# A spectral filter beside a gated MLP: the complex product made whole before the way back, and the inverse rows taken through memory

## The chip, the cores and the metric

The kernel runs on one core of a Trainium2 chip. The metric is the device time of one execution in microseconds (us). The engines are named as in the profile: PE is TensorE's matmul, PEld its weight load, DVE is VectorE, ACT is ScalarE, POOL is GpSimd and SP is SyncE, which issues nearly all transfers (DMAs). They run side by side; each takes its own instructions in order and waits on semaphores.

## The reference

```python
x = A_x                                   # (1, 2048, 512), bf16
xn = _layernorm(x, axis=-1)
# _A_ref: spectral filter
X = jnp.fft.rfft2(xn.astype(jnp.float32), axes=(-2, -1))
X = X * (w_r + 1j * w_i)                  # (2048, 257)
A = jnp.fft.irfft2(X, s=(2048, 512), axes=(-2, -1)).astype(jnp.bfloat16)
# _B_ref: GeGLU
g = jnp.einsum("bsd,df->bsf", xn, w_gate) # w_gate, w_up: (512, 1792)
u = jnp.einsum("bsd,df->bsf", xn, w_up)
B = jnp.einsum("bsf,fd->bsd", _gelu(g) * u, w_down)
return x + A + B
```

The output is the input plus a two-dimensional Fourier filter of the normalized input plus a gated MLP of it.

## The kernel before, in words

The 2048 rows lie as 16 tiles (index j) of 128 partitions. The MLP is cut into units for PE. A GeGLU unit (`geglu_unit`, line 490) makes 128 hidden features of 512 rows: four matmuls of 512 columns for the gate and four for the up projection (L504), the GELU on ACT (L516) and the product with the up half on DVE into hT (L524). A down unit (`down_unit`, L552) is fourteen matmuls of 512 columns for one tile of rows, added to x by DVE (L558). After the first tiles, 66 such units are left in one list; `filler(n)` issues the next n of it. They are written by hand between the units of the spectral path, so that PE has work while that path waits for other engines. There is no planner: the order in which the program issues operations is the order on every engine, and dependencies become semaphore waits.

The spectral path factors the transform of length 2048 into 64 times 32 parts. `unit_A` (L574) and `unit_d` (L600), sixteen each, transform along the long factor and along the columns; the result goes to memory and back in two parts (`shuffle`, L619), which swaps the order of the indices. Then comes the loop that the change rewrites. It has 16 units of two groups each (32 groups, 257 columns of the half spectrum):

- `unit_B(u)` does two matmuls (L635) with the constant BM, which finish the forward transform. ACT copies the pair of PSUM banks to Xc (L640). DVE multiplies Xc by the real filter into M1 (L643) and by the imaginary one into M2 (L644).
- `unit_c(u)` does, for each group, two matmuls that add in one bank: one constant times M1 (L656), another times M2 (L657). The second constant holds the turn by the imaginary unit, so the complex product becomes whole only in this sum. ACT copies the pair to Vp (L662), and four transfers per unit (L667) spread it over the partitions of V.

A row of Xc holds one of four components (real or imaginary part, of a frequency or of its mirror) of one of 2 times 16 indices; before the change the component lies in the low bits of the row number (`row_c`, line 89). Sixteen `unit_e` (L683) and sixteen `unit_fin` (L704) go back along the two axes, and DVE and POOL add the result to x (L714 to L722). Every finished tile is stored by SP (L536).

The loop has 18 passes; pass u issues `unit_c(u - 2)`, `unit_B(u)` and one or two fillers, 19 in all. Two more fillers follow, then the loop over `unit_e` and `unit_fin` with one filler in each of 16 passes, and four down units at the end. PSUM has 8 banks: three for the GeGLU units, four for the spectral units, one for the down units. Xc, M1, M2 and Vp have two buffers each. The transfers of V wait for Vp and for the last `unit_A`, because V shares its buffer with `unit_A`'s input.

Of the kernel before, what the change touches and what calls it, by code (L numbers as in the profile page):

```python
# [8 lines left out]
ALU = mybir.AluOpType  # L9
# [23 lines left out]
def _build_constants():  # L33
# [26 lines left out]

    AM = np.zeros((P, NJ, P))
# [3 lines left out]
    for j in range(NJ):  # L65
        th = pi2 * np.outer(16.0 * p + j, e) / S
        AM[:, j, 0:64] = np.cos(th)
        AM[:, j, 64:128] = -np.sin(th)
        AM[:, j, 64] = alt
        EM[0:64, j, :] = 2.0 * np.cos(th.T)  # L70
        EM[64:128, j, :] = -2.0 * np.sin(th.T)
        EM[0, j, :] = 1.0
        EM[64, j, :] = alt

# [8 lines left out]
    def idx(comp, e2):  # L83
        return slice(comp * 32 + e2 * 16, comp * 32 + e2 * 16 + 16)
# [4 lines left out]
    def row_c(comp, e2):  # L89
        return 8 * jj + comp * 2 + e2  # L90
# [26 lines left out]

    CM = np.zeros((P, 2, 2, P))
    wi = np.conj(w)
    for kind in range(2):  # L120
        M = CM[:, kind, 0, :]
# [19 lines left out]
        for e2 in range(2):  # L141
            for re, im in ((0, 1), (2, 3)):
                CM[row_c(re, e2), kind, 1, :] = M[row_c(im, e2), :]
                CM[row_c(im, e2), kind, 1, :] = -M[row_c(re, e2), :]

# [8 lines left out]
class _Sched:  # L154
# [14 lines left out]
    def total(self, stream):  # L169
        return (stream, self.stream_cnt[stream])  # L170
# [59 lines left out]
def bass_parallel_sum__spectral_gfnet__glu_gated_geglu__prompt_kernel(  # L230
# [21 lines left out]
    with ExitStack() as es:  # L252

        def sb(name, shape, dt=BF16):
            return es.enter_context(nc.sbuf_tensor(name, shape, dt))
# [22 lines left out]
        Xc = [sb("Xc%d" % i, [P, 2, NK]) for i in range(2)]  # L278
        M1 = [sb("M1_%d" % i, [P, 2, NK]) for i in range(2)]
        M2 = [sb("M2_%d" % i, [P, 2, NK]) for i in range(2)]  # L280
# [18 lines left out]
        CM = small[:, 3 * P:7 * P].rearrange("p (k t q) -> p k t q", k=2, t=2)  # L299
# [18 lines left out]
        def sp_bank_bf(slot):  # L318
# [12 lines left out]
                                      "w0", "w1", "w2", "w3", "dr0", "dr1", "perm1", "perm2_0", "perm2_1", "out")]  # L331
# [42 lines left out]
        d1 = nc.dram_tensor("stage_p", [NJ, P, 512], BF16).ap()  # L374

        def load_filter(name, dst, src):
            for q in range(4):
                e2 = q % 2
                load(name, dst[q:P:8, :, :], src.rearrange("(c h) k -> c h k", h=P)[:, 32 * e2:32 * e2 + 32, :])

                g0 = 1 - e2
                mirror = bass.AP(tensor=src.tensor, offset=src.offset + (P - 32 * e2 - g0) * NK,
                                 ap=[[P * NK, 16], [-NK, NG - g0], [1, NK]])
                load(name, dst[q + 4:P:8, g0:NG, :], mirror)
                if e2 == 0:
                    load(name, dst[q + 4:P:8, 0, :], src.rearrange("(c h) k -> c h k", h=P)[:, 64, :])
            spec[name] = [total(name)]
# [234 lines left out]
        Xc_readers = [[], []]  # L622
        M_readers = [[], []]
        Vp_readers = [[], []]
        ev_M = {}

        def unit_B(u):
            s2 = u % 2
# [11 lines left out]
            ev_c = sch.op("act", lambda e: e.activation(Xc[s2][:], sp_pair(slot), ACT.Copy), deps=[ev_p] + Xc_readers[s2])  # L640
            ring_sp.add_reader(slot, ev_c, 2)
            md = [ev_c] + M_readers[s2]
            a = sch.op("dve", lambda e: e.tensor_tensor(M1[s2][:], Xc[s2][:], wr_sb[:, 2 * u:2 * u + 2, :], ALU.mult), deps=md + spec["wr"])  # L643
            b = sch.op("dve", lambda e: e.tensor_tensor(M2[s2][:], Xc[s2][:], wi_sb[:, 2 * u:2 * u + 2, :], ALU.mult), deps=md + spec["wi"])  # L644
            Xc_readers[s2] = [a, b]
            ev_M[u] = [a, b]

        def unit_c(u):
# [3 lines left out]
            def f_c(e):  # L652
                ins = None
                for i in range(2):
                    kind = 1 if 2 * u + i == 0 else 0
                    e.matmul(sp_bank(slot + i)[:, 0:NK], CM[:, kind, 0, :], M1[s2][:, i, :], start=True, stop=False)  # L656
                    ins = e.matmul(sp_bank(slot + i)[:, 0:NK], CM[:, kind, 1, :], M2[s2][:, i, :], start=False, stop=True)  # L657
                return ins

            ev_p = sch.op("pe", f_c, deps=ev_M[u] + bdeps)  # L660
# [3 lines left out]
            for i in range(2):  # L664
                g = 2 * u + i
                for pq in range(2):
                    sch.op("sp", lambda e, g=g, i=i, pq=pq: e.dma_start(V[g:P:32, :, pq * HD:(pq + 1) * HD],  # L667
                                                                       Vp[s2][pq * 64:pq * 64 + 64, i, pq:pq + HD]),
                           deps=[ev_v, spec["A_last"]], stream="perm2_%d" % s2)
            Vp_readers[s2] = [total("perm2_%d" % s2)]  # L670
            spec["perm2_%d" % s2] = total("perm2_%d" % s2)
# [5 lines left out]
        def unit_e(j):  # L677
# [8 lines left out]
            ev_p = sch.op("pe", f_e, deps=[spec["perm2_0"], spec["perm2_1"], spec["eg"]] + bdeps)  # L686
# [123 lines left out]
        filler(5)  # L810

        spare = todo["left"] - 18 - 2 - 16 - 4
        for u in range(18):
            if u >= 2:
                unit_c(u - 2)
            if u < 16:
                unit_B(u)
            filler(1 + (u + 1) * spare // 18 - u * spare // 18)
        filler(2)
# [58 lines left out]
```

## Time and profile before

| | |
|---|---|
| median of 3 runs | 186.47 us (186.15 to 186.47) |
| the profiled execution | 186.33 us |
| its span, first to last instruction | 184.5 us |
| busy PE / DVE / ACT / POOL in the span | 180.1 / 109.6 / 88.0 / 55.4 us |
| `unit_B` matmuls L635 | 32 |
| `unit_c` matmuls L656, L657 | 32 and 32, 7.9 us of records each |
| products L643, L644 | 16 each, 428 and 422 ns |
| ACT copies Xc L640, Vp L662 | 16 each, 595 and 599 ns |
| transfers Vp to V (L667) | 64, 32.0 KB each |
| first `unit_B` to the end of the last `unit_c` | 77.35 to 121.21 us |

The busy times overlap, since the engines run side by side. Records of matmuls overlap as well: a matmul's record is longer than the distance to the next one's start, so the distances between starts tell what one costs. A line of the waits names who waited, for whom, and then the us in total, the number of times and the longest. A line of the order of time has the start, the length, the engine, the line and the operation, and in brackets the idle time before it with what ended it. The transfers' lines end in the number of issues, the KB of each and the median us from issue to landing.

### The profile page before, as it was taken

The page shows a single profiled execution, that of the slowest core. Times are in us where ns is not written, and L with a number is a line of the kernel's source. Part 1 is how long each engine was busy: PE and PEld are TensorE (multiplying, and loading weights), DVE is VectorE, ACT ScalarE, POOL GpSimd, SP SyncE. Part 2 cuts the span into 40 slices and gives each one's busy share as a digit, 9 for nine tenths or more (in the row PEclk, how much of TensorE's full clock was granted, in tenths as well). Part 3 has the DMA queues.
Part 4 walks back from the last instruction along what each step waited for, and adds up shares of the span by engine and source line. Part 5 has one row for each costly group of instructions (what it writes and reads, how often), then busy time and mean ns, then how long its engine had stood idle before and what let it go on. Part 6 is the DMA issues. An engine that isn't in the chain of part 4 may idle for free.

```text
span 184.5 us, 3257 instructions
## 1 busy us (share of the span) xinstructions
PE 180.1 (98%) x1197; PEld 103.6 (56%) x1197; DVE 109.6 (59%) x232; ACT 88.0 (48%) x161; POOL 55.4 (30%) x54
## 2 busy tenths in 40 slices
PE   7999999999999999999999999999999999998994
PEld 7788455565655544455555555554455555555453
DVE  2768968798674624365464654623266768688421
ACT  2644357777462633165475464523263635566000
POOL 0073290393720000000000000000049679699900
PEclk9999999999999999999999999999999999999999
DMA  5999972999994918301112112111001110111001
GB/s 152 352 365 373 373 233 82 164 189 262 197 203 153 290 64 236 134 0 52 46 47 52 51 50 54 46 41 27 5 0 57 54 63 28 57 59 34 28 28 57
DMA packets 25441, 21.95 MB, mean 119 GB/s; under 512 B 1617, under 2 KB 24657, under 8 KB 25297
## 3 DMA queue, kind: packets, MB, share of 16 engines
q1 hardware_dynamic: 24752, 21.32, 42.4%
q10 hardware_dynamic: 672, 0.43, 0.8%
q8 instruction: 9, 0.15, 0.4%
q14 instruction: 8, 0.06, 0.1%
HBM read 15.45 MB, written 4.19 MB: 106 GB/s over the span
## 4 chain that ended last, share of the span: by engine, by line
PE 93%; DMA 4%; SPq 1%; ACT 0%; issue 0%; DVE 0%
PE ps L504 51%; PE ps L552 26%; DMA wu_sb<-in_B_w_up_dram 4%; PE ps L574 2%; PE ps L683 2%; PE ps L600 2%; PE ps L635 2%; PE ps L657 2%; PE ps L656 2%; PE ps L704 2%; PE ps L441 2%; SPq L338 1%; ACT bufA L688 0%; DVE x_sb L558 0%
## 5 line engine op out<-in xcount | busy, mean ns | idle before, releaser
L504 PE MATMUL ps<-xnT,wg_sb 128*128 128x512 bf16 (+1 forms) x248 | 58.6, 359 | 0.3 <-DMA wu_sb<-in_B_w_up_dram 0.2
L504 PE MATMUL ps<-xnT,wu_sb 128*128 128x512 bf16 (+1 forms) x248 | 58.5, 359 | 0.0
L524 DVE TENSOR_TENSOR hT<-ps,gg 128x512 bf16<-128x512 f32 (+1 forms) x62 | 39.4, 637 | 19.7 <-PE ps L504 18.2
L552 PE MATMUL ps<-wd_sb,hT 128*128 128x512 bf16 (+1 forms) x238 | 50.5, 367 | 0.0
L516 ACT ACTIVATE gg<-ps 128x512 bf16<-128x512 f32 (+1 forms) x62 | 34.5, 556 | 23.2 <-PE ps L504 22.1
L718 POOL TENSOR_TENSOR bufC<-bufC 128x256 bf16<-128x256 f32 x16 | 14.7, 917 | 88.3 <-DVE bufC L715 88.3
L504 PEld LDWEIGHTS ps<-xnT,wu_sb 128*128 128x128 bf16 x248 | 24.2, 98 | 24.1
L552 PEld LDWEIGHTS ps<-wd_sb,hT 128*128 128x128 bf16 x238 | 22.9, 98 | 22.6
L504 PEld LDWEIGHTS ps<-xnT,wg_sb 128*128 128x128 bf16 x248 | 22.9, 98 | 15.8 <-DMA wu_sb<-in_B_w_up_dram 0.5
L558 DVE TENSOR_TENSOR x_sb<-ps,x_sb 128x512 bf16<-128x512 f32 (+1 forms) x17 | 11.2, 660 | 26.1 <-PE ps L552 26.1
L722 POOL TENSOR_TENSOR x_sb<-x_sb,bufC 128x512 bf16<-128x512 bf16 x16 | 18.7, 1169 | 2.3
L465 POOL TENSOR_TENSOR bufC<-bufA 128x1024 bf16<-128x1024 bf16 x8 | 16.8, 2124 | 7.9 <-DVE bufA L423 7.9
L662 ACT ACTIVATE Vp<-ps 128x514 bf16<-128x514 f32 x16 | 9.6, 599 | 19.1 <-DMA bufB<-Vp 10.9
L688 ACT ACTIVATE bufA<-ps 128x512 bf16<-128x512 f32 x16 | 9.6, 597 | 16.3 <-PE ps L683 16.3
L608 ACT ACTIVATE bufA<-ps 128x512 bf16<-128x512 f32 x16 | 11.9, 744 | 9.2 <-PE ps L600 9.2
L643 DVE TENSOR_TENSOR M<-Xc,wr_sb 128x514 bf16<-128x514 bf16 x16 | 6.9, 428 | 15.4 <-ACT Xc L640 15.4
L400 DVE BATCH_NORM_STATS2 st<-x_sb 128x6 f32<-128x512 bf16 x16 | 10.9, 680 | 2.4 <-DMA x_sb<-in_A_x_dram 2.3
L640 ACT ACTIVATE Xc<-ps 128x514 bf16<-128x514 f32 x16 | 9.5, 595 | 4.0 <-PE ps L635 4.0
L714 DVE TENSOR_TENSOR bufC<-bufC,ps 128x256 f32<-128x256 f32 x16 | 6.7, 421 | 5.7 <-ACT bufC L711 5.7
L657 PE MATMUL ps<-M,small 128*128 128x257 bf16 x32 | 7.9, 274 | 0.0
L656 PE MATMUL ps<-M,small 128*128 128x257 bf16 x32 | 7.9, 274 | 0.0
L415 POOL TENSOR_SCALAR rstd<-ag 128x4 f32<-128x4 f32 (+1 forms) x4 | 1.6, 402 | 20.4 <-DVE ag L401 20.4
(42 smaller groups left out, 142.5 us busy)
## 6 DMA issues: line engine op xcount, KB each, us to landing
stage_p<-bufA SPq DMA_DIRECT2D x16, 128.0 KB, 5.9
bufC<-stage_p SPq DMA_DIRECT2D x4, 512.0 KB, 5.0
bufB<-Vp SPq DMA_DIRECT2D x64, 32.0 KB
out_dram<-x_sb SPq DMA_DIRECT2D x15, 128.0 KB, 1.7
wd_sb<-in_B_w_down_dram SPq DMA_DIRECT2D x1, 1792.0 KB, 14.2
wr_sb<-in_A_w_r_dram SPq DMA_DIRECT2D x6, 257.0 KB, 5.9
wi_sb<-in_A_w_i_dram SPq DMA_DIRECT2D x6, 257.0 KB, 9.7
x_sb<-in_A_x_dram SPq DMA_DIRECT2D x3, 512.0 KB, 9.9
```

Source lines behind the costliest of these rows:

```text
L400: ev = sch.op("dve", lambda e: e.bn_stats(st[:, j, :], x_sb[:, j, :]), deps=[ev_x[j]])
L465: ev_hf[m] = [sch.op("pool", lambda e, t=t, op=op: e.tensor_tensor(half[:, m, t, :, :], rows[:, 0, :, :], rows[:, 1, :, :], op), deps=deps ...
L504: ins = e.matmul(gu_bank(slot)[:, 0:w], wsb[:, dc, fc * P:(fc + 1) * P], xnT[:, dc, b * 512 + a:b * 512 + a + w], start=(dc == 0), stop=(d ...
L516: ev_gg = sch.op("act", lambda e: e.activation(gg, gu_bank(gslot)[:, 0:w], ACT.Gelu_apprx_tanh), deps=[ev_gm] + gg_readers[s2])
L524: ev_h = sch.op("dve", lambda e: e.tensor_tensor(hT[hb][:, fc, a:a + w], gu_bank(uslot)[:, 0:w], gg, ALU.mult), deps=[ev_um, ev_gg] + hdeps)
L552: ins = e.matmul(bank(slot)[:, 0:w], hT[hb][:, fc, jj * P:(jj + 1) * P], wd_sb[:, fc, cs], start=(fc == 0), stop=(fc == NFC - 1))
L558: ev_a = sch.op("dve", lambda e, slot=slot, cs=cs: e.tensor_tensor(x_sb[:, j, cs], bank(slot)[:, 0:w], x_sb[:, j, cs], ALU.add), deps=[ev_ ...
L608: ev_T[j] = sch.op("act", lambda e: e.activation(dst, src, ACT.Copy), deps=[ev_p, tr[j]] + ev_hf[j // 4])
L656: e.matmul(sp_bank(slot + i)[:, 0:NK], CM[:, kind, 0, :], M1[s2][:, i, :], start=True, stop=False)
L657: ins = e.matmul(sp_bank(slot + i)[:, 0:NK], CM[:, kind, 1, :], M2[s2][:, i, :], start=False, stop=True)
L718: y = [sch.op(("dve", "pool")[h], lambda e, h=h, op=op: e.tensor_tensor(rS[s2][:, h * HD:(h + 1) * HD], yeS[s2][:, 0, :], yeS[s2][:, 1, :] ...
L722: ev_o = sch.op("pool", lambda e: e.tensor_tensor(x_sb[:, j, :], x_sb[:, j, :], rS[s2], ALU.add), deps=[a, b, ev_xn[j]] + ev_acc.get(j, []))
```

## The change

The complex product is made whole on DVE, and the way back gets one matmul per group. For that the rows are put in another order: partitions 0 to 63 now hold the real parts and 64 to 127 the imaginary parts. Two transfers per unit copy Xc with its halves exchanged into a new buffer JX. DVE multiplies Xc by the real filter into M1, multiplies JX by the imaginary filter in place, and adds the two into M1. The sign of the turn is put into the filter: four operations (`negate`) turn the sign of wi on the first 64 partitions, ahead of the loop. The filters are loaded in the new order, with the same number of transfers. The second half of the constant CM goes. Xc and JX have three buffers each.

The result Vp is no longer spread over V by four transfers per unit. One transfer per unit writes it to memory (`stage_g`), and in three steps, for 12, 12 and 8 groups, two transfers each (`back`) read it to V. The rows of V come out in another order, which `idx` and the constant EM follow.

The loop has 19 passes: pass u issues `unit_c(u - 3)`, `unit_B(u)`, the product of unit u - 2, and one filler as long as u is under 15. `back` follows in passes 10, 16 and 18. Six fillers stand after the loop. The four operations `negate` stand among the five fillers ahead of the loop.

```diff
+    EM = EM.reshape(2, 2, NG, NJ, P).transpose(2, 0, 1, 3, 4)
...
     def idx(comp, e2):
-        return slice(comp * 32 + e2 * 16, comp * 32 + e2 * 16 + 16)
+        r = comp % 2 * 64 + e2 * 32 + comp // 2 * 16
+        return slice(r, r + 16)
...
     def row_c(comp, e2):
-        return 8 * jj + comp * 2 + e2
+        return comp % 2 * 64 + 4 * jj + comp // 2 * 2 + e2
...
         def load_filter(name, dst, src):
-            for q in range(4):
-                e2 = q % 2
-                load(name, dst[q:P:8, :, :], src.rearrange("(c h) k -> c h k", h=P)[:, 32 * e2:32 * e2 + 32, :])
...
+            for ri in range(2):
+                for e2 in range(2):
+                    plus, minus = (slice(64 * ri + 2 * pm + e2, 64 * ri + 64, 4) for pm in range(2))
+                    load(name, dst[plus, :, :], src.rearrange("(c h) k -> c h k", h=P)[:, 32 * e2:32 * e2 + 32, :])
...
+        def negate(i):
+
+            w = wi_sb[0:64, 8 * i:8 * i + 8, :]
+            spec.setdefault("neg", []).append(
+                sch.op("dve", lambda e: e.tensor_scalar(w, w, -1.0, None, ALU.mult), deps=spec["wi"]))
...
+        PARTS = ((0, 12), (12, 24), (24, 32))
...
         def unit_B(u):
...
-            a = sch.op("dve", lambda e: e.tensor_tensor(M1[s2][:], Xc[s2][:], wr_sb[:, 2 * u:2 * u + 2, :], ALU.mult), deps=md + spec["wr"])
-            b = sch.op("dve", lambda e: e.tensor_tensor(M2[s2][:], Xc[s2][:], wi_sb[:, 2 * u:2 * u + 2, :], ALU.mult), deps=md + spec["wi"])
-            Xc_readers[s2] = [a, b]
-            ev_M[u] = [a, b]
+            ev_Xc[u] = sch.op("act", lambda e: e.activation(Xc[s3][:], sp_pair(slot), ACT.Copy), deps=[ev_p] + Xc_readers[s3])
+            ring_sp.add_reader(slot, ev_Xc[u], 2)
+            for h in range(2):
+                sch.op("sp", lambda e, h=h: e.dma_start(JX[s3][64 * h:64 * h + 64, :, :], Xc[s3][64 - 64 * h:128 - 64 * h, :, :]),
+                       deps=[ev_Xc[u]] + JX_readers[s3], stream="jx%d" % s3)
+            ev_JX[u] = total("jx%d" % s3)
+            Xc_readers[s3] = [ev_JX[u]]
+
+        def product(u):
+
+            s2, s3 = u % 2, u % 3
+            gs = slice(2 * u, 2 * u + 2)
+            a = sch.op("dve", lambda e: e.tensor_tensor(M1[s2][:], Xc[s3][:], wr_sb[:, gs, :], ALU.mult), deps=[ev_Xc[u]] + M_readers[s2] + spec["wr"])
+            b = sch.op("dve", lambda e: e.tensor_tensor(JX[s3][:], JX[s3][:], wi_sb[:, gs, :], ALU.mult), deps=[ev_JX[u], spec["neg"][u // 4]])
+            ev_Y[u] = sch.op("dve", lambda e: e.tensor_tensor(M1[s2][:], M1[s2][:], JX[s3][:], ALU.add), deps=[a, b])
+            Xc_readers[s3].append(a)
+            JX_readers[s3] = [ev_Y[u]]
 
         def unit_c(u):
...
-                    e.matmul(sp_bank(slot + i)[:, 0:NK], CM[:, kind, 0, :], M1[s2][:, i, :], start=True, stop=False)
-                    ins = e.matmul(sp_bank(slot + i)[:, 0:NK], CM[:, kind, 1, :], M2[s2][:, i, :], start=False, stop=True)
+                    ins = e.matmul(sp_bank(slot + i)[:, 0:NK], CM[:, kind, :], M1[s2][:, i, :], start=True, stop=True)
...
-            ev_p = sch.op("pe", f_c, deps=ev_M[u] + bdeps)
+            ev_p = sch.op("pe", f_c, deps=[ev_Y[u]] + bdeps)
...
-            for i in range(2):
-                g = 2 * u + i
-                for pq in range(2):
-                    sch.op("sp", lambda e, g=g, i=i, pq=pq: e.dma_start(V[g:P:32, :, pq * HD:(pq + 1) * HD],
-                                                                       Vp[s2][pq * 64:pq * 64 + 64, i, pq:pq + HD]),
-                           deps=[ev_v, spec["A_last"]], stream="perm2_%d" % s2)
...
+            part = next(i for i, (lo, hi) in enumerate(PARTS) if lo <= 2 * u < hi)
+            name = "vd%d_%d" % (part, s2)
+            sch.op("sp", lambda e: e.dma_start(d2[2 * u:2 * u + 2].rearrange("g r k -> r g k"), Vp[s2][:]), deps=[ev_v], stream=name)
+            Vp_readers[s2] = [total(name)]
+
+        def back(part):
+
+            lo, hi = PARTS[part]
+            ev = [total("vd%d_%d" % (part, i)) for i in range(2)]
+            for pq in range(2):
+                src = bass.AP(tensor=d2.tensor, offset=d2.offset + (lo * P + 16 * pq) * NK + pq,
+                              ap=[[32 * NK, 4 * (hi - lo)], [NK, NJ], [1, HD]])
+                sch.op("sp", lambda e, pq=pq, src=src: e.dma_start(V[4 * lo:4 * hi, :, pq * HD:(pq + 1) * HD], src),
+                       deps=ev + [spec["A_last"]], stream="perm2")
+            spec["perm2"] = total("perm2")
...
-        filler(5)
-
-        spare = todo["left"] - 18 - 2 - 16 - 4
-        for u in range(18):
-            if u >= 2:
-                unit_c(u - 2)
+        for i in range(4):
+            filler()
+            negate(i)
+        filler()
+        for u in range(19):
+            if u >= 3:
+                unit_c(u - 3)
             if u < 16:
                 unit_B(u)
-            filler(1 + (u + 1) * spare // 18 - u * spare // 18)
-        filler(2)
+            if 2 <= u < 18:
+                product(u - 2)
+            if u < 15:
+                filler()
+            if u in (10, 16, 18):
+                back((10, 16, 18).index(u))
+        filler(todo["left"] - 16 - 4)
```

## The prediction

> **What bounds the kernel now.** I read the page's busy times and its chain first, then the waits of every engine, then the order of time of one pass of the loop that the change rewrites, then the transfers, and last two stretches of the clock. All times are those of the profiled execution: 186.33 us, a span of 184.5 us and 1.8 us around it; it stands 0.14 us under the median of 186.47 us.
>
> ```profile
> span 184.5 us, 3257 instructions
> PE 180.1 (98%) x1197; PEld 103.6 (56%) x1197; DVE 109.6 (59%) x232; ACT 88.0 (48%) x161; POOL 55.4 (30%) x54
> ...
> PE 93%; DMA 4%; SPq 1%; ACT 0%; issue 0%; DVE 0%
> ```
> TensorE (PE) is busy 98% of the span and is 93% of the chain. Whatever shortens its list of work shortens the kernel, as long as it never waits.
>
> ```profile
> ACT Vp L662 <- DMA bufB<-Vp: 10.9, 9, 1.9
> ...
> PE ps L704 <- ACT bufA L688: 0.5, 1, 0.5
> ```
> In the waits, ScalarE (ACT) loses 10.9 us to the transfers out of Vp, while PE, apart from the start, waits 0.5 us in all. The transfers' wait hurts nobody.
>
> ```profile
> 116.04 0.27 PE L656 MATMUL ps<-M,small 128*128 128x257 bf16 x1
> ...
> 116.15 0.27 PE L657 MATMUL ps<-M,small 128*128 128x257 bf16 x1
> ...
> 116.25 0.69 DVE L524 TENSOR_TENSOR hT<-ps,gg 128x512 bf16<-128x512 f32 x1
> ...
> 116.48 0.39 PE L635 MATMUL ps<-bufC,small 128*128 128x257 bf16 x2
> ...
> 116.69 0.60 ACT L662 ACTIVATE Vp<-ps 128x514 bf16<-128x514 f32 x1 [0.71 <-PE ps L657]
> 116.71 1.02 PE L504 MATMUL ps<-xnT,wg_sb 128*128 128x512 bf16 x4
> 117.18 0.59 ACT L640 ACTIVATE Xc<-ps 128x514 bf16<-128x514 f32 x1
> ...
> 117.81 0.43 DVE L643 TENSOR_TENSOR M<-Xc,wr_sb 128x514 bf16<-128x514 bf16 x1 [0.87 <-ACT Xc L640]
> 118.15 0.42 DVE L644 TENSOR_TENSOR M<-Xc,wi_sb 128x514 bf16<-128x514 bf16 x1
> ...
> 118.43 0.27 PE L656 MATMUL ps<-M,small 128*128 128x257 bf16 x1
> ...
> 135.88 0.41 DVE L715 TENSOR_TENSOR bufC<-bufC,ps 128x256 f32<-128x256 f32 x1
> 136.33 0.42 DVE L718 TENSOR_TENSOR bufC<-bufC 128x256 bf16<-128x256 f32 x1
> ```
> One pass takes 2.39 us. The records of 0.27 us overlap: the starts lie 0.11 us apart, and that is what a 257-column matmul costs. A 512-column one costs 0.216 us (a GeGLU unit of eight is 1.73 us in the chain, a down unit of fourteen 3.02 us). VectorE (DVE) starts the hT product 0.21 us after PE has left the unit. Independent 514-column products start 0.34 us apart; one that needs the result before it starts 0.04 us after that one's end (135.88 + 0.41, then 136.33).
>
> ```profile
> out_dram<-x_sb SPq DMA_DIRECT2D x15, 128.0 KB, 1.7
> ...
> small<-c_small ACTq DMA_DIRECT2D x1, 32.0 KB, 2.3
> ```
> The nearest rows for a small transfer, issue to landing: 1.7 and 2.3 us.
>
> **The change part by part.**
>
> *Matmuls removed.* L657 goes: 32 matmuls at 0.11 us, all on the path, **-3.54 us**. Their weight loads (98 ns) lie beside the matmuls and give nothing more.
>
> *The longer way from B to C.* A product now needs Xc, two swap transfers, and three DVE operations of which the third waits for the second. Call E the moment when PE leaves a unit. DVE starts hT at E+0.21, its next operation 0.60 later (such a pair stands at 26.84 and 27.44), so the first multiply starts at E+0.81, the second at E+1.16, the add at E+1.62 (1.16 + 0.42 + 0.04), and Y is there at E+2.04. The C matmuls are wanted at the end of the next pass, E+2.17 (0.22 + 0.22 + 1.73). With 0.05 us to wake PE (ACT's end at 169.55, L704 at 169.60) that leaves 0.08 us: no wait, but hardly any cover. If the three operations take 0.3 us more, each pass in a row of GeGLU units costs about half of the excess. In the first three passes there is no C, the pass is 1.95 us, and the first C waits 2.09 - 1.95, **+0.14 us**.
>
> *The swaps.* Xc(u) ends 1.51 us into its pass (PE ends C after 0.39, ACT starts Vp at 0.41, Xc at 0.91). Two issues at 0.45 us (L338 shows 0.43, L667 up to 0.67) and a landing of 2.0 us, between the 1.7 and the 2.3, give the swapped copy at 4.0 us. The multiply by wi wants it two passes on, at 4.34 + 1.16 = 5.5 us. So 1.5 us of cover hides them within the loop; beyond that DVE waits, hT behind it waits, and PE a little later.
>
> *The end of the loop.* Fifteen passes carry a filler; passes 15 to 18 carry none. This is what I find decisive. Take E as the moment after the last filler. PE does C(12) and B(15), 0.44 us, and then has only C(13), C(14), C(15), each behind DVE:
> C(13): Y(13) at 2.04, so C at 2.09, idle 1.65 us.
> C(14): multiplies at 1.96 and 2.31, add at 2.77, Y at 3.19, C at 3.24; C(13) ended at 2.31, idle 0.93 us.
> C(15): B(15) was read out by 1.51; swaps issued at 1.55 and 2.04, landed at 4.04; multiply at 4.07, add at 4.53, Y at 4.95, C at 5.00; C(14) ended at 3.46, idle 1.54 us.
> Together **+4.12 us**. The bounds: with swaps that are never late, C(15)'s multiply starts at 3.47 and the idle time is 3.52 us; with issues of 0.66 us (L667) and a landing of 2.7 us (the last of a group of Vp transfers issued at 95.31, its waiter started at 98.04) Y(14) is late too, C(15) starts at 6.04 and the idle time is 5.16 us.
>
> *Fillers moved.* Before, 19 units lay in the loop and 2 after it; now 15 and 6. The same 21, so E(0) stands behind the same work. It also needs the last return through memory: Vp(15) 1.0 us after C(15), its write 0.5 + 2.7, two reads at 0.66 each and 5.8 us (the largest landing of the 512 KB reads of stage_p), 11.3 us. Seven units (six GeGLU, one down) give 13.4 us. Hidden; without this cover PE would wait the difference ahead of E(0).
>
> *Queues.* SP loses 64 issues of 0.53 us (43 us of its time) and gets 54. Each swap waits on SP behind the Vp write of the same pass, whose ACT work ends 0.5 us earlier. The return reads of the first part (786 KB) go out after pass 10 and the swaps of pass 11 run behind them: at the rate of the stage_p reads (1 MB between 68.64 and 74.97) they are done some 6 us after issue, about 8.5 us into pass 10; the copy is wanted at 7.7, and the down unit of pass 13 gives 1.3 more. Nothing, with 0.5 us to spare. ACT's 10.9 us of waits go, and nothing comes of it, since PE did not wait for ACT.
>
> *Nothing on the path.* Four negations of 2056 columns: at most four times the 0.34 us of L423, 1.4 us each, between hT operations that leave DVE 1.03 us idle; hT comes up to 0.8 us late there, and its bank is wanted 0.5 us later still, a down unit follows. Filter loads: the same 20 issues on other partitions, landing up to 11.3 us after 45.2, wanted at 69.9. 64 KB less of constants.
>
> *Sum.* -3.54 + 0.14 + 4.12 = +0.72: 186.33 + 0.72 = 187.05, **187.0 us**. With the hole of 3.52 us it is +0.12, with that of 5.16 us +1.76: 186.4 to 188.1 us.
>
> *The clock.* What speaks against a hole in PE's work most:
> ```profile
> 177.56:180.97 3.41, 3.41 (x26) 2.44 (x25) 1.03 (x2) 0.00 (x0) 0.00 (x0) 1.00 0.20 68
> 180.97:184.38 3.41, 1.15 (x11) 0.78 (x8) 0.51 (x2) 0.00 (x0) 0.00 (x0) 1.00 0.16 48
> 184.40:184.54 0.14, 0.00 (x0) 0.00 (x0) 0.00 (x0) 0.00 (x0) 0.00 (x0) 0.50 0.00 0
> ```
> In these answers by stretch the columns after the length are the busy times of PE, its weight loads, DVE, ACT and GpSimd, then the granted clock. PE worked 1.15 us of the stretch that ends at 184.38, and then the clock is 0.50. At the start 36 matmuls of 128 columns take 4.03 us, 0.11 each, against 0.055 in the loop at L683: a slow start that lasts to about 6.9 us. In the new hole PE would work 1.1 of 5.2 us. [...]
>
> **The rivals.**
> *The clock halves after the hole.* For it: 1.15 us of work in 3.41 us were too few at the end. Against it: there the work had stopped for good, here some comes every microsecond. The price by the rows: the slow start from 0.97 to 6.9 us loses half of 5.9, at most 3.0 us; part of it would fall into the hole, so 2.0 us: 187.0 + 2.0 = 189.0 us.
> *DVE or the swaps hold PE in the middle of the loop as well.* The cover is 0.08 us. Three operations 0.3 us longer cost about 0.11 us in each of some nine GeGLU passes, or one return read delays a swap by 1 us beyond its cover: 188.1 us. Against it: the operations have the forms of L643, whose sixteen records lie between 427 and 430 ns.
> *Faster: DVE makes a product sooner, at the end of the loop.* One product takes it 1.15 us in the walk (0.35 + 0.46 + 0.34), three in a row set the lower bound of the hole. At 0.9 us each the hole is 3 x 0.25 shorter, 2.77 us: 186.33 - 3.54 + 0.14 + 2.77 = 185.7 us. It decides from a hole of under 3.4 us (3.54 - 0.14). For it: no operand is in PSUM. Against it: neither is one in L643 and L644, whose starts lie 0.34 us apart, and the swap would have to land 1.1 us after its second issue, where the nearest row has 1.7.
>
> **How the numbers follow.** 0.2% (0.37 us) is about what a measurement of this kernel tells from no change. The held clock with the hole: 0.50, 187.0 us, its own range 186.4 to 188.1, a quarter of it within 0.37 us of before. The halved clock: 0.34, 188.3 to 190. The middle of the loop: 0.10. Faster: 0.06. So faster 0.06, same 0.13, slower 0.81. The range leaves out the faster case with the lowest edge of the first, and the upper end of the halved clock: 186.5 to 189.5 us.
>
> **What the profile after would show.** L657's line gone and a C pair 0.22 us; between the last loop filler and the next filler three waits of PE for DVE, of 1.6, 0.9 and 1.5 us, the last with DVE itself waiting for the swap; no PE wait between passes 4 and 14; no wait ahead of E(0); ACT without its 10.9 us. A PEclk digit under 9 behind the hole is the second case. I am wrong if PE stands still elsewhere, or if the hole is under 3 us.

## The result and the profile after

The changed kernel takes 193.36 us (median of 4 runs, 192.74 to 196.48) against 186.37 us for the kernel before on the same chip (186.15 to 186.47): the ratio is 1.0365, with an interval of 1.0336 to 1.0395. Forecast were 187.0 us and a range up to 189.5 us. The sign is right, the size is not.

The execution profiled for the result (196.48 us) lies apart from the three others (192.74 to 193.52 us), so the profile shown here is that of the same kernel in the run `r1_again`: 194.82 us, a span of 193.0 us.

From its page, the busy times, the slices of PE, DVE and the clock, and the chain:
```profile
span 193.0 us, 3188 instructions
PE 180.2 (93%) x1146; PEld 100.9 (52%) x1165; DVE 117.6 (61%) x252; ACT 88.7 (46%) x161; POOL 55.5 (29%) x54
...
PE   7889999999999999999999926699999999998994
...
PEclk9999999999999999999999987579999999999999
...
PE 84%; DMA 9%; SPq 2%; DVE 2%; ACT 1%; issue 1%
```
PE's share of the chain fell from 93% to 84%, and transfers went from 4% to 9%. Thirty-two matmuls are gone, and yet PE is busy for 180.2 us, as before (180.1): in four slices, from 111 to 130 us, the clock's digits are 8, 7, 5 and 7, and the matmuls there last longer (a GeGLU unit of eight takes 3.04 us from 115.59 on, 1.74 us from 101.63 on).

Its waits (who, for whom: us in total, times, longest):
```profile
ACT Vp L682 <- DMA stage_g<-Vp: 7.3, 2, 5.6
PE ps L677 <- DVE M L665: 6.8, 4, 3.4
...
DVE JX L664 <- DMA JX<-Xc: 5.4, 2, 4.9
```
PE waits four times at L677 (`unit_c`), and one wait has 3.4 us of the 6.8. Behind it stands a wait of DVE of 4.9 us for a swap. The order of time shows the place:
```profile
103.76 1.14 SPq L696 DMA_DIRECT2D bufB<-stage_g  x2
...
105.56 1.12 SPq L654 DMA_DIRECT2D JX<-Xc  x2
...
113.65 0.43 DVE L664 TENSOR_TENSOR JX<-JX,wi_sb 128x514 bf16<-128x514 bf16 x1 [4.89 <-DMA JX<-Xc]
...
114.11 0.43 DVE L665 TENSOR_TENSOR M<-M,JX 128x514 bf16<-128x514 bf16 x1
...
114.60 0.56 PE L677 MATMUL ps<-M,small 128*128 128x257 bf16 x2 [3.43 <-DVE M L665]
...
120.54 0.40 PE L677 MATMUL ps<-M,small 128*128 128x257 bf16 x2 [1.48 <-DVE M L665]
...
121.68 0.61 PE L677 MATMUL ps<-M,small 128*128 128x257 bf16 x2 [0.74 <-DVE M L665]
...
123.47 0.61 PE L677 MATMUL ps<-M,small 128*128 128x257 bf16 x2 [1.18 <-DVE M L665]
```
The first part's return reads go out at 103.76, the swaps of unit 11 follow at 105.56. The multiply that needs them starts only at 113.65, and C(11) at 114.60, 3.6 us after the end of the down unit ahead of it. The last three lines are the forecast hole, C(13) to C(15). In the chain the second swap of unit 11 is one step:
```profile
106.08 7.55 DMA JX<-Xc
```
A swap lands in 2.1 us at the median; this one took 7.55. The same reads hold back the Vp writes: ACT waits 5.6 us for one, up to 113.05, which is 0.6 us before the multiply starts. And by stretches of the clock (length, then busy PE, weight loads, DVE, ACT, GpSimd, then the granted clock):
```profile
111.28:114.69 3.41, 0.09 (x1) 0.10 (x2) 1.01 (x3) 1.09 (x2) 0.00 (x0) 1.00 0.49 121
114.69:118.10 3.41, 3.41 (x11) 1.50 (x11) 1.55 (x4) 1.69 (x3) 0.00 (x0) 0.50 0.48 128
118.10:121.52 3.42, 1.36 (x9) 0.50 (x6) 2.79 (x7) 1.64 (x3) 0.00 (x0) 1.00 0.29 75
121.52:124.93 3.41, 2.07 (x7) 0.86 (x8) 1.29 (x4) 0.94 (x3) 0.00 (x0) 0.50 0.63 98
124.93:128.34 3.41, 3.41 (x10) 1.22 (x8) 0.69 (x1) 0.91 (x2) 0.00 (x0) 0.50 1.10 250
```
After a stretch in which PE worked 0.09 us, one at half clock; after one with 1.36 us, two. In the three halved ones PE works 3.41 + 2.07 + 3.41 = 8.9 us, at full clock 4.45.

So the execution adds up: 186.3 (before) - 3.54 (matmuls) + 0.15 (first C) + 3.6 (C(11)) + 4.17 (the hole, measured below) + 4.4 (clock) = 195.1, against 194.82. It has three halved stretches and a mean clock of 0.973. Five of the eight executions of this kernel have 0.982, which makes two halved stretches and, estimated from the first and last of these three, about 1.7 us less: 193.4, near the median of 193.36.

### The profile page after: what moved, and what is told of

It is laid out like the page before. It is cut to its first block, busy times and chain, and to the rows that moved or that the text cites. A ratio compares the mean times of both kernels' runs of the same rounds, so it can differ in the third digit from the quotient of the medians.

```text
span 194.7 us, 3207 instructions
## 1 busy us (share of the span) xinstructions
PE 182.8 (94%) x1165; PEld 102.0 (52%) x1165; DVE 117.7 (60%) x252; ACT 88.8 (46%) x161; POOL 55.4 (28%) x54
## 4 chain that ended last, share of the span: by engine, by line
PE 87%; DMA 7%; DVE 2%; ACT 1%; SPq 1%; issue 0%
PE ps L504 50%; PE ps L552 23%; DMA JX<-Xc 5%; PE ps L441 2%; PE ps L574 2%; PE ps L710 2%; PE ps L600 2%; PE ps L731 2%; PE ps L677 2%; DMA x_sb<-in_A_x_dram 2%; PE ps L646 1%; PE ps L485 1%; DVE hT L524 1%; ACT Xc L651 1%; SPq L654 0%; DVE JX L664 0%
## 5 line engine op out<-in xcount | busy, mean ns | idle before, releaser
L504 PE MATMUL ps<-xnT,wg_sb 128*128 128x512 bf16 (+1 forms) x248 | 61.6, 373 | 0.0
L504 PE MATMUL ps<-xnT,wu_sb 128*128 128x512 bf16 (+1 forms) x248 | 60.3, 367 | 0.0
L504 PEld LDWEIGHTS ps<-xnT,wu_sb 128*128 128x128 bf16 x248 | 24.9, 100 | 25.6 <-issue 2.2
L504 PEld LDWEIGHTS ps<-xnT,wg_sb 128*128 128x128 bf16 x248 | 23.9, 101 | 17.1 <-issue 2.2
L677 PE MATMUL ps<-M,small 128*128 128x257 bf16 x32 | 6.9, 300 | 7.5 <-DVE M L665 7.5
L664 DVE TENSOR_TENSOR JX<-JX,wi_sb 128x514 bf16<-128x514 bf16 x16 | 6.8, 422 | 6.1 <-DMA JX<-Xc 6.1
L677 PEld LDWEIGHTS ps<-M,small 128*128 128x128 bf16 x32 | 2.7, 99 | 12.1 <-DVE M L665 11.2
```

What stands on the lines that cost most here:

```text
L504: ins = e.matmul(gu_bank(slot)[:, 0:w], wsb[:, dc, fc * P:(fc + 1) * P], xnT[:, dc, b * 512 + a:b * 512 + a + w], start=(dc == 0), stop=(d ...
L677: ins = e.matmul(sp_bank(slot + i)[:, 0:NK], CM[:, kind, :], M1[s2][:, i, :], start=True, stop=True)
```

## The experiments

Theory: the first return reads make the swaps behind them late (a wait of 3.6 us), the forecast hole at the end of the loop costs its 4.2 us, and each of the two holes halves the clock for a while. Rivals: the swaps are late for another reason than the reads; the late swap is one more of many small delays of DVE; the halved clock adds nothing that the waits don't already explain.

**The kernel again, and the two causes apart.** `r1_again` is the changed kernel itself.

> The changed kernel itself once more, for a profile of an ordinary execution. Both theories: 192.7 to 193.6 us, a wait of PE for the product in pass 14 of about 4 us (C(11) behind the swap of unit 11), three waits of about 1.5, 0.7 and 1.2 us at the end of the loop, and two stretches of 3.4 us at half the clock.

Measured: 193.86 us (193.3 to 194.82), ratio 1.0413 (1.0375 to 1.0452), 0.3 us above what was expected. Its profile is the one above: the waits are as expected, the halved stretches are three and not two.

`r2_few_reads` shrinks the first two parts' return reads to one group each, so the rest of those rows of V is not read back and the output is not the filter's; everything else stays.
```diff
             lo, hi = PARTS[part]
             ev = [total("vd%d_%d" % (part, i)) for i in range(2)]
+            if part < 2:
+                hi = lo + 1
```


> The reads of V for the parts 0 and 1 are cut to one group each, so most of V isn't filled and the output isn't the filter's. Theory 1 (the return reads ahead of the swaps hold the loop): the 4.1 us wait in pass 14 and the half clock behind it (up to 1.7 us) go, 187.2 to 188.8 us, with the waits at the end of the loop as they were. Rival (the loop waits for something else, such as the product's DVE work): still a wait in pass 14, over 190 us.

`r3_filled` keeps the reads and closes the hole: four of the six fillers behind the loop go into its passes 15 to 18.
```diff
-            if u < 15:
-                filler()
+            filler()
```


> Passes 15 to 18 get a filler each, so two instead of six stand after the loop. Theory: the three waits at the end of the loop go (4 us, and the half clock there), the wait in pass 14 stays, and E(0) now waits for the last return reads, by about 3 us (10 us needed, four units of 1.73 us to cover): 190 to 191 us. Rival (the hole is not what costs, the clock falls for other reasons): above 192 us.

`r4_both` has both edits.

> Both edits: the reads of parts 0 and 1 cut to one group each (output incomplete) and fillers in all passes. If these two are the whole loss and 32 matmuls are worth 3.5 us: 186.4 - 3.5 + 0.1 + 2 to 3 (E(0) waiting for the last reads) = 185 to 186 us, below the kernel before. Rival (the shorter matmul list gains nothing): above 187 us.

Measured:

| kernel | median us (lowest to highest) | ratio to before (interval) |
|---|---|---|
| `r1_again` | 193.86 (193.3 to 194.82) | 1.0413 (1.0375 to 1.0452) |
| `r2_few_reads` | 188.51 (188.09 to 189.07) | 1.0123 (1.0102 to 1.0144) |
| `r3_filled` | 188.69 (187.47 to 190.8) | 1.0109 (1.0052 to 1.0165) |
| `r4_both` | 184.19 (184.0 to 184.57) | 0.9891 (0.9877 to 0.9906) |

By these medians each edit alone takes 5.2 to 5.4 us, both together 9.7. With both the time is 2.1 us under before (with most of V not read back), and the matmuls' 3.54 are there to be seen. `r3_filled` and `r4_both` came out below what was expected of them: the wait ahead of E(0) was shorter than the 2 to 3 us expected (below), and in two executions of `r3_filled` the clock held.

Without the long reads only the hole is left. The order of time of `r2_few_reads` from the last B on:
```profile
112.97 0.38 PE L646 MATMUL ps<-bufC,small 128*128 128x257 bf16 x2
...
114.83 0.40 PE L677 MATMUL ps<-M,small 128*128 128x257 bf16 x2 [1.47 <-DVE M L665]
...
115.96 0.40 PE L677 MATMUL ps<-M,small 128*128 128x257 bf16 x2 [0.74 <-DVE M L665]
...
117.80 0.61 PE L677 MATMUL ps<-M,small 128*128 128x257 bf16 x2 [1.45 <-DVE M L665]
```
The starts lie 1.86, 1.13 and 1.84 us apart, less the 0.22 us that a pair costs: 1.64, 0.91 and 1.62, together 4.17 us. The forecast walk had 1.65, 0.93 and 1.54, together 4.12. The stretches of the same kernel:
```profile
113.66:117.07 3.41, 0.79 (x4) 0.23 (x4) 2.73 (x8) 1.80 (x4) 0.00 (x0) 1.00 0.45 120
117.07:120.48 3.41, 2.68 (x8) 1.17 (x9) 0.64 (x2) 0.92 (x2) 0.00 (x0) 0.50 0.41 89
120.48:123.89 3.41, 3.36 (x17) 1.51 (x17) 1.38 (x2) 0.87 (x2) 0.00 (x0) 1.00 0.31 84
```
Three waits, none over 1.7 us, suffice for a halved stretch, and all four executions have one (mean clock 0.99). PE works 2.68 us in it and loses half of that, 1.34 us: 186.3 - 3.54 + 0.15 + 4.17 + 1.34 = 188.4.

With the hole filled only the late swap is left. The waits of `r3_filled`, and its stretch behind them:
```profile
PE ps L677 <- DVE M L665: 3.8, 1, 3.8
...
PE ps L710 <- DMA bufB<-stage_g: 1.7, 1, 1.7
```
```profile
112.34:115.75 3.41, 0.66 (x5) 0.51 (x6) 1.58 (x4) 1.32 (x3) 0.00 (x0) 1.00 0.34 94
115.75:119.16 3.41, 3.41 (x10) 1.36 (x9) 1.15 (x4) 1.46 (x3) 0.00 (x0) 0.50 0.38 97
...
132.80:136.20 3.40, 1.67 (x11) 0.76 (x11) 0.69 (x1) 0.93 (x2) 0.00 (x0) 1.00 0.47 99
```
The profiled execution took 190.8 us. By the mean clocks one more (189.63 us) has a halved stretch, and two have none (187.47 and 187.75 us, mean clock 1.000); how long PE waited in those two, no trace shows. The fillers gone from behind the loop also uncover the last return: 1.7 us ahead of E(0) (the first `unit_e`), in `r4_both` 0.9 us.

**What the halved clock costs.** The sums above take it from the stretches. `s4_busy` takes it away: it is `r2_few_reads` with matmuls on the identity matrix, 128 columns each and used by nobody, put into the hole.
```diff
+            if u > 15:
+                busy((22, 11, 18)[u - 16])
             if u >= 3:
                 unit_c(u - 3)
```


> As r2_few_reads (reads of parts 0 and 1 cut, output incomplete), with matmuls of 128 columns that nobody reads put into the three waits at the end of the loop: 22, 11 and 18 of them, 1.2, 0.6 and 1.0 us. Theory (the clock halves because PE does too little in a stretch of 3.4 us): the clock stays at 1.0 and the time falls by the 1.2 to 1.7 us of the slow stretch, from 188.5 to about 187 us. Rival (the half clock costs nothing that the waits don't cover): 188.5 us, no change.

Measured: 187.17 us (187.07 to 187.25), ratio 1.0042 (1.0027 to 1.0057), 1.34 us less than `r2_few_reads`; the C matmuls still come when DVE is ready. In this stretch of 4 us PE is busy for most of the hole, and the clock holds:
```profile
114.00:118.00 4.00, 3.45 (x52) 2.88 (x49) 3.27 (x10) 1.92 (x4) 0.00 (x0) 1.00 0.45 117
```
So about 1.3 us is what the halved clock costs behind the hole alone, as half of 2.68 says; that the two figures agree to the hundredth is chance, since the executions of `r2_few_reads` spread over 1 us.

**Why the first reads are slow: their size, their destination or their rows in memory.** The packet records in the trace, averaged over the data packets of 512 bytes, give 64 to 65 ns for the first reads of the changed kernel, against 29 to 31 for the reads of stage_p that the forecast took its rate from. The stage_p reads go to all partitions, the first part's to partitions 0 to 47. Three kernels with all passes filled, the reads cut into four parts of 8 groups, and two down units at the end in place of four; `s1_parts4` is that alone:
```diff
-        PARTS = ((0, 12), (12, 24), (24, 32))
+        PARTS = ((0, 8), (8, 16), (16, 24), (24, 32))
...
-            if u < 15:
-                filler()
-            if u in (10, 16, 18):
-                back((10, 16, 18).index(u))
-        filler(todo["left"] - 16 - 4)
+            filler()
+            if u in (8, 12, 16, 18):
+                back((8, 12, 16, 18).index(u))
+        filler(todo["left"] - 16 - 2)
```


> Fillers in all passes, four after the loop, and the last two passes of the loop over E take two of the four down units that stood at the end. The return reads are cut into four parts of 8 groups (512 KB each, on 32 neighbouring partitions) in passes 8, 12, 16 and 18. Theory (a swap stands behind whatever reads were issued before it): a read of 512 KB at the 140 KB/us of the first part lasts 3.7 us instead of 5.6, the wait for the swap falls from 3.4 us to 0 to 1.7 us per part: 184 to 186.5 us. Rival (each read costs the same fixed stall): two waits of about 3.5 us, over 188 us.

`s2_spread4` sends each part to every fourth partition (EM follows), on top of it:
```diff
-                sch.op("sp", lambda e, pq=pq, src=src: e.dma_start(V[4 * lo:4 * hi, :, pq * HD:(pq + 1) * HD], src),
+                sch.op("sp", lambda e, pq=pq, src=src: e.dma_start(V[part:P:4, :, pq * HD:(pq + 1) * HD], src),
```


> As s1_parts4, but the rows of V are ordered so that each part goes to every fourth partition, as the reads of stage_p do, with the constant EM in the same order. If 48 neighbouring partitions are what makes a packet of 512 B take 60 to 88 ns instead of 27 to 30: packets of about 30 ns, reads landing within 4.3 us, no wait for a swap, 183 to 184 us. Rival (the source in memory is the cause): packets and waits as in s1_parts4.

`s3_aligned` is `s1_parts4` with rows 1024 bytes apart in memory and no offset of one element:
```diff
-        d2 = nc.dram_tensor("stage_g", [NG, P, NK], BF16).ap()
+        d2 = nc.dram_tensor("stage_g", [NG, P, 512], BF16).ap()
```


> As s1_parts4, but the rows of stage_g stand 1024 B apart, and the reads of the second half start at column 0 instead of 1, so that every packet of 512 B starts on a multiple of 1024 B (half of V is shifted by one column, the output is not the filter's). If the odd place in memory makes the packets slow: about 30 ns each, landing within 4.3 us and 183 to 184 us. Rival (the partitions): as s1_parts4.

Measured: 185.13 us (184.22 to 185.46), ratio 0.9926 (0.9903 to 0.995); 184.65 us (184.31 to 184.99), 0.9913 (0.9892 to 0.9934); 184.42 us, 0.9894 (0.9877 to 0.9911). The packets took 37 to 38 ns in `s1_parts4` (43 in its third part), 29 to 30 in `s2_spread4` (36 in its third part) and 35 to 38 in `s3_aligned`, where 30 had been expected if the rows' place mattered. It does not; the destination does, for the packets. The time of `s2_spread4` missed its 183 to 184 us. The transfers' lines of `r1_again`, then of the three (issues, KB of each, median us to landing):
```profile
bufB<-stage_g SPq DMA_DIRECT2D x4, 384.0 KB, 6.3
```
```profile
bufB<-stage_g SPq DMA_DIRECT2D x8, 256.0 KB, 4.3
```
```profile
bufB<-stage_g SPq DMA_DIRECT2D x8, 256.0 KB, 3.4
```
```profile
bufB<-stage_g SPq DMA_DIRECT2D x8, 256.0 KB, 4.2
```
In time the three are alike: their intervals overlap. Eight groups at a time, in passes 8 and 12, leave the swaps hardly late (their longest landing is 3.8 us in `s1_parts4`), and PE's waits at L677 are 0.4 to 0.6 us in all.

**Is it the queue?** The swaps stand behind the reads on SP. If the order of the queue alone made them late, reads issued elsewhere would free them. `s5_pool` issues the reads from GpSimd, `s6_act` from ACT, with the three parts of the change and the fillers of `s1_parts4`.
```diff
-                sch.op("sp", lambda e, pq=pq, src=src: e.dma_start(V[4 * lo:4 * hi, :, pq * HD:(pq + 1) * HD], src),
+                sch.op("act", lambda e, pq=pq, src=src: e.dma_start(V[4 * lo:4 * hi, :, pq * HD:(pq + 1) * HD], src),
```


> Fillers as in s1_parts4; the return reads in the changed kernel's three parts (12, 12 and 8 groups, 48 and 32 neighbouring partitions), but issued by GpSimd instead of SP. Theory (a swap is late because it stands behind the reads in SP's own queue): beside them on another queue the swaps of passes 11 and 12 land within about 4 us instead of 7.5, the wait of 3.4 to 3.8 us shrinks to under 1 us: 184.5 to 186 us. Rival (the reads fill the 16 transfer engines, whatever the queue): swaps as late as before, 187.5 us and more.

> As s5_pool, with the reads issued by ACT. Same two cases; on top, two issues of about 0.5 us stand between ACT's copies in pass 10, which puts a GELU about 1 us late: 184.5 to 186.5 us if the queue is the cause, 187.5 us and more if the engines are.

Measured: 187.58 us (186.73 to 189.04, 10 runs), ratio 1.0077 (1.0049 to 1.0105), and 192.09 us, ratio 1.0297 (1.0268 to 1.0327). The swaps' own lines, and PE's waits, of `s5_pool` and of `s6_act`:
```profile
DMA to landing us min/median/max: 1.9/2.3/6.3
...
PE ps L677 <- DVE M L665: 2.8, 3, 1.4
```
```profile
DMA to landing us min/median/max: 1.9/2.2/8.4
...
PE ps L677 <- DVE M L665: 4.7, 1, 4.7
```
A queue of their own does not free the swaps: `s6_act` meets the rival, and the theory that the place in SP's queue is the whole cause falls. ACT waits for no Vp write there, so the late swap alone makes PE wait. The time of `s5_pool` meets the rival by 0.1 us, its waits lie between the two cases: in the profiled execution, which took 186.73 us, PE waits three times, at most 1.4 us. Its reads are not the same transfers, either: issued from GpSimd they came as packets of 4096 bytes and not of 512. The packet records tell the cases of `r1_again` and `s6_act` apart. In `r1_again` no packet of a swap (1028 bytes) begins between 105.0 and 110.0 us, while the reads' packets run from 104.98 to 111.40; the first comes at 110.42, the others follow together with the queued Vp writes, and the second swap of unit 11 lands at 113.63. In `s6_act` the reads go out at 102.58 and meet the swaps of unit 10, issued at 102.61 and 103.11. Swap packets begin at 105.2, beside the reads, but up to 110.0 only 132 of them do, two swaps' worth, where 64 make one. So in both cases the reads take the transfer engines (the DMA share, the last column but one of these answers, is 1.25 in `r1_again` from 109 to 110 us and 1.21 in `s6_act` from 107.57 to 110.98), on one queue by order and on two by sharing. Why the share of the swaps is so small was not settled: half of them write to low partitions, too, and no run has swaps that don't.

**The destination alone.** `t1_every2` is `r3_filled` with the first two parts sent to every second partition of 0 to 95, the sizes and passes of the reads unchanged.
```diff
-                sch.op("sp", lambda e, pq=pq, src=src: e.dma_start(V[4 * lo:4 * hi, :, pq * HD:(pq + 1) * HD], src),
+                sch.op("sp", lambda e, pq=pq, src=src: e.dma_start(V[part:4 * NJ + 32:2, :, pq * HD:(pq + 1) * HD] if part < 2 else V[96:P, :, pq * HD:(pq + 1) * HD], src),
```


> As r3_filled (three parts of 12, 12 and 8 groups, 786 KB in the first), but the rows of V are ordered so that the first two parts go to every second partition of 0 to 95 instead of 48 neighbouring ones. If the neighbouring partitions make the packets slow: 30 to 40 ns instead of 64, the swap of pass 11 lands in about 4.5 us instead of 7.9, the wait in pass 14 falls from 3.8 to under 1.5 us, 184.5 to 186 us. Rival (the size of the part, three rows to an engine): 60 ns, the same wait, 187.5 us or more.

Measured: 190.49 us (188.97 to 191.24), ratio 1.0194 (1.0134 to 1.0254). The packets meet the expectation; the wait misses it by a little (under 1.5 us was expected), the longest landing of a swap by 1 us (5.6 us, about 4.5 expected), and the time by far. The first read's packets fell from 64 to 39 ns, DVE's wait for the swap from 5.2 to 3.3 us and PE's in the middle of the loop from 3.8 to 1.8 us (the lines are one later in this kernel):
```profile
PE ps L711 <- DMA bufB<-stage_g: 2.4, 1, 2.4
...
PE ps L678 <- DVE M L666: 1.8, 1, 1.8
```
So between these two executions the destination is worth 2.0 us of the wait; that the size of the reads makes the other 1.8 us is likely, but was not shown. What the kernel gained there it lost elsewhere: the wait ahead of E(0) is 2.4 us (1.7 in `r3_filled`) and the clock fell behind it, and in the profiled execution also between 7.2 and 10.6 us, at the start, where nothing was changed. The sum of the profiled execution, 190.65 us, is 186.4 (before) - 3.54 + 0.15 + 1.8 + 2.4 + half of the 3.21 and 3.42 us that PE works in the two halved stretches, 3.3, = 190.5. By the mean clocks (0.991 and 0.982) every execution of `t1_every2` has one or two halved stretches, those of `r3_filled` none or one. That the spread destination alone makes the kernel faster is therefore not shown; what it does to the packets and to the waits is.

**Versions that beat both kernels.** With the reads in four spread parts, three kernels move the fillers between the loop, the stretch behind it and the end. `b1_three_end` is `s2_spread4` with one filler fewer behind the loop and one down unit more at the end; `b2_three_end13` also makes the second return in pass 13 instead of 12; `b3_four_end13` goes one filler further, and so has two behind the loop and the change's four down units at the end:
```diff
-            if u in (8, 12, 16, 18):
-                back((8, 12, 16, 18).index(u))
-        filler(todo["left"] - 16 - 2)
+            if u in (8, 13, 16, 18):
+                back((8, 13, 16, 18).index(u))
+        filler(todo["left"] - 16 - 4)
```


> As s2_spread4, but three fillers after the loop and three down units at the very end (s2_spread4: four and two, where DVE's last sums wait 4.4 us for GpSimd). E(0) has 4.9 us to spare in s2_spread4 and loses one unit of it (3.0 us at most). Theory (the end of the kernel waits for the last rows' sums): 0.4 to 0.8 us less than s2_spread4, 183.9 to 184.3 us. Rival (the end is not exposed): 184.6 us.

> Between b1_three_end and b3_four_end13: three fillers after the loop, three down units at the end, the second part's read in pass 13. If the 0.7 us that PE waits for the last read in b3_four_end13 is the only loss left there: it goes, and the end costs some 0.3 us: 183.6 to 184.2 us. Rival (the end costs as much as the read): 184.1 to 184.6 us.

> Two fillers after the loop, all four down units at the end as before the change, and the second part's read one pass later, in pass 13, which carries a down unit. The wait of 0.55 us for a swap in s2_spread4 should go, and the end is as before the change; E(0) has 0 to 0.2 us to spare: 183.3 to 184.2 us. Rival (E(0) waits for the last read): 184.5 us or more, with a wait of PE for the read.

Measured: 184.59 us (ratio 0.9892, 0.9865 to 0.992), 184.56 us (0.9892, 0.9864 to 0.992) and 184.06 us (183.55 to 185.22; 0.9871, 0.9828 to 0.9915). The first two hit their rivals and not their expectations, and the rivals disagree: by that of `b1_three_end` the end of the kernel is not exposed, by that of `b2_three_end13` it costs as much as the read. `b3_four_end13` lies in its expected range, but with the wait for the last read that its rival named. The intervals of the three overlap, so they are not told apart, and what the end costs stays open; all beat the kernel before by 1 to 1.3%. PE's waits in `b3_four_end13`:
```profile
PE ps L710 <- DMA bufB<-stage_g: 0.7, 1, 0.7
...
PE ps L677 <- DVE M L665: 0.2, 1, 0.2
```
The 3.54 us of matmuls are paid for with 0.9 us of waits there; the rest of the difference to 2.4 us gained was not looked for.

## Why the prediction was right and wrong

- **The matmuls removed** (-3.54 us): right. `r4_both` has no hole and no late swap and stands 2.1 us under before; 186.3 - 3.54 + 0.15 for the first C, + 0.9 ahead of E(0) and 0.7 more than before of waiting for the weights at the start give 184.5, against 184.57 for the profiled execution.
- **The longer way from B to C**: right. The first C waited 0.15 us (0.14 forecast), and no ordinary pass waits: the cover of 0.08 us was enough.
- **The swaps** (landing 2.0 us, hidden): right for a swap that has the transfers to itself, 2.1 us at the median.
- **The end of the loop** (+4.12 us): right, 4.17 us in `r2_few_reads`, gap by gap.
- **Queues: "Nothing, with 0.5 us to spare."** This step failed, and with the halved clock behind it it is the larger part of the miss: without the long reads 5.4 us go (`r2_few_reads`). It is also the sign of being wrong that the prediction named, PE standing still elsewhere than at the end of the loop. It had the right place: the first part's return reads ahead of the swaps of pass 11. It had them done some 6 us after issue, from the rate of the stage_p reads. Their last packet came 111.40 - 103.76 = 7.6 us after issue, since a packet took 64 ns and not the 30 of those reads: 1.6 us more. (By the packets alone it would be an estimated 3.2 us, 34 ns for each of 1536 packets on 16 engines; the 6 us held some slack, since they allow three quarters of the bytes nearly the 6.3 us of the whole.) And the step took the end of the reads for the arrival of the swap; but the swaps' packets, and queued Vp writes, began only at 110.42, when the reads were ending, and the second swap landed 113.63 - 111.40 = 2.2 us after the last of the reads. 1.6 + 2.2 - 0.5 to spare = 3.3 us, against 3.6 measured. The rival of the middle of the loop had priced just this, "one return read delays a swap by 1 us beyond its cover", at 0.10 and a third of its size.
- **The clock**: the sum took the held clock, and what the prediction had against the halved one was that in the hole "some comes every microsecond". That choice was wrong: in `r2_few_reads` PE worked 0.79 us of the 3.41 us that hold most of the first gap, the second and the start of the third, none of the three over 1.7 us, and half clock followed. Behind the hole alone it costs 1.34 us (`s4_busy`), which puts the case at 188.5 us, near the rival's 189.0, to which 0.34 had been given. With the late swap as a second hole it costs 4.4 us in the execution above.
- **Fillers moved** (hidden, 11.3 of 13.4 us): right, `r1_again` has no wait ahead of E(0). The price named for losing that cover is what `r3_filled` and `r4_both` then paid, 1.7 and 0.9 us.

Forecast 187.05 us for the profiled execution; 3.6 for the queues and 4.4 for the clock make 195.05. Had the Queues step been right, the clock alone would have left the time at about 188.5 us, as `r2_few_reads` shows, inside the range. The range fell because two cases that were priced as alternatives came together, and because the one that was given 0.10 was three times its size.

## What to carry to other kernels

Where a small transfer that a compute engine waits for runs behind bulk ones, add the small one's whole landing to the end of the bulk (here the swap landed 2.2 us after the last of the reads), and take the bulk's rate from a row with the same set of destination partitions, not only the same size of packet (here 64 ns for 512 bytes to 48 neighbouring partitions, 30 to all). Several short waits close together are to be priced as one hole for the clock, as the three of `r2_few_reads` show, which cost 4.17 us, and the clock behind them 1.34 more (`s4_busy`): add PE's work over a window of the length that the profile shows, 3.41 us here, and if it is as low as in the stretches before the halved ones of the loop (0.09 to 1.36 us; no sharp bound was found), add the loss of the halved window. And before a change that frees PE is judged, look whether the freed time needs other work moved into it: here the same change is 4% slower or 1% faster, by where a few fillers stand and how the reads are cut.

## What the hardware showed unexpectedly

**Where a read landed changed its rate.** Data packets of 512 bytes out of memory, all on SP's queue: 64 ns to 48 neighbouring partitions from 0 on, 44 ns to partitions 48 to 95, 35 to 39 ns to 32 neighbouring ones, 39 ns to every second one of 0 to 95, 29 to 30 ns to every fourth of 128 (43 and 36 ns in the third parts of `s1_parts4` and `s2_spread4`). In GB/s while such reads ran, the last column, of `r1_again` and of `s2_spread4`:
```profile
109.00:110.00 1.00, 1.00 (x7) 0.47 (x5) 0.00 (x0) 0.00 (x0) 0.00 (x0) 1.00 1.25 124
```
```profile
100.00:101.00 1.00, 1.00 (x8) 0.54 (x6) 0.08 (x1) 0.00 (x0) 0.00 (x0) 1.00 1.03 293
```
Why one set of partitions is slower than another was not shown. Nor does the destination alone make the 44 ns: the same partitions 48 to 95 took 36 ns with the reads on ACT's queue (`s6_act`), and the second part of `t1_every2`, spread like its first, took 46 ns where the first took 39. Vp writes ran beside these parts and the slower third parts above, but also beside the ends of faster ones; what makes the difference was not settled.

**Another issuing engine was not another road.** A swap beside the reads took up to 8.4 us with the reads on ACT's queue and 6.3 on GpSimd's (in packets of 4096 bytes), against 7.5 on the same queue.

**How little idle time halved the clock.** Changes of the clock in these traces lie on a grid of 3.413 us (in `r1_again` 5.46 + 32 x 3.413 = 114.69 us). Of the grid's stretches at full clock shown above, the ones with PE busy 0.09, 0.66, 0.79 and 1.36 us were followed by half clock, the one with 1.67 us was not; at half clock, 2.07 us of work (0.61) did not bring it back, 2.68 (0.79) and 3.41 did. By these the bound would lie between 0.40 and 0.49 of a stretch. But this stretch near the start of `t1_every2` has PE busy for 0.55 of it, and half clock followed. Its matmuls are others, 24 of 128 columns in short groups, nearly all on a buffer of zeros (`warm_up`):
```profile
3.79:7.20 3.41, 1.87 (x24) 1.22 (x22) 2.53 (x7) 1.44 (x2) 0.00 (x0) 1.00 1.04 337
```
So PE's busy time alone does not set the bound for every kind of work, and what else counts was not found. It also stays open why one wait of 3.8 us halved the clock in the profiled execution of `r3_filled` and two other executions show no halved clock; where the wait falls on the grid may decide it.
